# More units convolved channel-major: taps alternating on VectorE, broadcast multiplies on GpSimd

## The chip, the cores and the metric

The kernel runs on one core of one Trainium2 chip. The metric is the device time of one execution in microseconds; the executions of one kernel in the same rounds lay 0.15 to 0.65% apart, from the fastest to the slowest. Versions are compared in the same rounds on the same chip. "Step" below is one of the 768 pairs of matmul groups that make a gate and a val tile; twelve steps are a block of 512 tokens, and 48 steps, four blocks, are a unit.

## The reference

A causal depthwise convolution of seven taps, whose weights are a softmax per head, feeds a gated feed-forward block.

```python
w = exp(weight - max) ; w = w / (sum(w) + 1e-09)          # 8 heads x 7 taps
x_unf = x_pad[:, idx, :].reshape(B, S, K, H, group)       # x: 8 x 4096 x 192
out = einsum('hk,bskhg->bshg', w, x_unf)
g = out @ w_gate                                          # 192 -> 1536
silu = g * (1.0 / (1.0 + exp(-g)))
y = (silu * (out @ w_val)) @ w_out                        # 1536 -> 192
```

## The kernel before

Each step does six matmuls into a gate and a val bank (three of each), ScalarE takes the silu of gate, VectorE multiplies it by val, and TensorE multiplies the products h by w_out in groups between triples of steps ("acc").

The convolution of the next units is done beside that, in one of two ways. On TensorE, a banded matmul ("cv") is copied out as tm, written to DRAM and fetched back transposed as xc. Channel-major, a transposed load puts channels on partitions, so that a tap is a multiply by a scalar per partition. A unit takes six jobs; in the kernel before, unit 3 and every second one after it went this way:

```python
POOLED = range(3, NU, 2)
ON_DVE, ON_ACT, ON_POOL = (0, 1), (2, 3, 4), (5, 6)       # the seven taps of a job
def on_dve(k):
    nc.vector.scalar_tensor_tensor(total, shifted(k), tap[:, k:k+1],
                                   zero if k == 0 else total, op0=mult, op1=add)
def on_act(k):
    nc.scalar.activation(part, shifted(k), AF.Copy, scale=tap[:, k:k+1])
    add(part, k)                                          # GpSimd: total += part
def on_pool(k):
    nc.gpsimd.tensor_scalar(part, shifted(k), scalar1=tap[:, k:k+1], op0=mult)
    add(part, k)
# ... one ScalarE tap, and with two of three also a VectorE tap, at steps 1, 7 and 10 of a block
# ... place(): four DMA copies arrange a finished block as pxc, what the gate matmuls read
...
if n == 23:
    make_channel_taps()          # masks on VectorE, then a tap matmul on TensorE at once
```

## Time and profile before

| | before |
|---|---|
| median | 792.3 us (791.2 to 792.6) |
| TensorE / VectorE / ScalarE / GpSimd busy | 99% / 80% / 74% / 57% |
| silu starts, first of unit 0 to first of unit 1 | 60.6 us |
| a later unit, without and with convolution on TensorE | 46.9 and 48.3 us |

The lines on which the argument rests are in the prediction. What the convolution costs the helpers is in the page's costliest groups (count, busy us, mean ns of one, idle time ahead of it and what ended it):

```profile
L636 POOL TENSOR_TENSOR total<-total,part 128x512 f32<-128x512 f32 x126 | 160.1, 1270 | 225.9 <-DVE total L619 174.1
...
L649 POOL TENSOR_SCALAR piece<-x,tap_c 128x512 f32<-128x512 f16 x84 | 137.9, 1641 | 0.0
L643 ACT ACTIVATE part<-x,tap_c 128x512 f32<-128x512 f16 x126 | 89.9, 714 | 3.7 <-DMA x<-xs 3.1
...
L619 DVE SCALAR_TENSOR_TENSOR total<-x,tap_c,fill 128x512 f32<-128x512 f16 x42 | 41.1, 979 | 2.4 <-DMA x<-xs 2.4
...
L619 DVE SCALAR_TENSOR_TENSOR total<-x,tap_c,total 128x512 f32<-128x512 f16 x42 | 31.4, 748 | 3.5 <-POOL total L636 3.5
```

The two VectorE rows do the same arithmetic on the same sizes; one is 979 ns because 15 of its 42 took about 1.4 us, each of them begun inside a GpSimd add.

### The profile page before, as it was taken

Reading aid. Unit: us, or ns where it says so; the run is one execution under the profiler, and the core shown is the slowest. Engines: PE = TensorE matmul, PEld = TensorE weight load, DVE = VectorE, ACT = ScalarE, POOL = GpSimd, SP = SyncE. Lnnn points to the kernel's source line nnn. Section 1 sums busy time; section 2 is a strip of 40 time slices with the busy share of each in tenths; the row PEclk is TensorE's granted clock in tenths of the full one; section 3 lists DMA queues with packets and bytes.
Section 4 is the critical chain, followed back from the end, with each engine's and each line's share of the span. In section 5 each row is a group of like instructions: output and inputs, shape, how many; then the busy total and the mean of one; then the engine's idle time right before and its main releaser. Section 6 shows DMA issues by size and latency. Waiting matters only on the chain.

```text
span 788.7 us, 28107 instructions
## 1 busy us (share of the span) xinstructions
PE 778.3 (99%) x11563; PEld 600.3 (76%) x11563; DVE 627.3 (80%) x988; ACT 584.7 (74%) x1010; POOL 453.3 (57%) x375
## 2 busy tenths in 40 slices
PE   8898999999999999999999999999999999999998
PEld 5665678886788767887678876888678886788886
DVE  7666888688887888778897788877888788897775
ACT  6566778678777787777787687777787777786664
POOL 8204669455793658926689166873669546684000
PEclk9999999999999999999999999999999999999999
DMA  9996668653585444853557625674257652531111
GB/s 144 152 165 130 136 134 149 136 109 80 111 151 124 94 108 102 168 118 62 129 116 135 137 63 118 129 152 110 56 134 135 145 117 59 119 93 44 42 42 42
DMA packets 175970, 88.49 MB, mean 112 GB/s; under 512 B 115898, under 2 KB 175170, under 8 KB 175170
## 3 DMA queue, kind: packets, MB, share of 16 engines
q1 hardware_dynamic: 147634, 69.57, 38.3%
q0 software_dynamic: 28208, 17.13, 16.4%
q8 instruction: 90, 1.47, 0.8%
q14 instruction: 38, 0.31, 0.1%
HBM read 34.26 MB, written 39.37 MB: 93 GB/s over the span
## 4 chain that ended last, share of the span: by engine, by line
PE 96%; SPq 1%; ACT 1%; DVE 0%; DMA 0%; issue 0%; ACTq 0%
PE gate L740 51%; PE acc L766 32%; PE val L740 11%; PE cv L462 1%; SPq L498 1%; PE warm L841 1%; SPq L520 0%; PE turn L431 0%; DMA x<-xs 0%; PE cv L373 0%; ACT sig L749 0%; PE acc L787 0%; DVE h L751 0%; ACT tme L391 0%; ACT wide L331 0%
## 5 line engine op out<-in xcount | busy, mean ns | idle before, releaser
L751 DVE TENSOR_TENSOR h<-sig,val 128x512 f16<-128x512 f16 x768 | 503.5, 686 | 144.9 <-PE val L740 93.6
L749 ACT ACTIVATE sig<-gate 128x512 f16<-128x512 f32 x768 | 458.2, 597 | 176.1 <-PE val L740 104.0
L740 PEld LDWEIGHTS <-w 64*128 64x128 f16 x4608 | 321.8, 110 | 125.4 <-issue 2.9
L766 PEld LDWEIGHTS <-h 64*128 64x128 f16 x6096 | 275.8, 94 | 45.7 <-issue 4.0
L766 PE MATMUL acc<-wo,h 64*128 64x192 f16 x6096 | 306.1, 243 | 2.1 <-ACT sig L749 2.1
L740 PE MATMUL val<-xc,w 64*128 64x512 f16 x1296 | 306.9, 378 | 0.0
L740 PE MATMUL gate<-xc,w 64*128 64x512 f16 x1296 | 306.9, 378 | 0.0
L636 POOL TENSOR_TENSOR total<-total,part 128x512 f32<-128x512 f32 x126 | 160.1, 1270 | 225.9 <-DVE total L619 174.1
L740 PE MATMUL val<-pxc,w 64*128 64x512 f16 x1008 | 236.6, 376 | 0.0
L740 PE MATMUL gate<-pxc,w 64*128 64x512 f16 x1008 | 236.6, 376 | 0.0
L649 POOL TENSOR_SCALAR piece<-x,tap_c 128x512 f32<-128x512 f16 x84 | 137.9, 1641 | 0.0
L643 ACT ACTIVATE part<-x,tap_c 128x512 f32<-128x512 f16 x126 | 89.9, 714 | 3.7 <-DMA x<-xs 3.1
L636 POOL TENSOR_TENSOR total<-total,piece 128x512 f32<-128x512 f32 x42 | 54.2, 1290 | 3.5
L619 DVE SCALAR_TENSOR_TENSOR total<-x,tap_c,fill 128x512 f32<-128x512 f16 x42 | 41.1, 979 | 2.4 <-DMA x<-xs 2.4
L636 POOL TENSOR_TENSOR pxc<-total,piece 128x512 f16<-128x512 f32 x28 | 36.1, 1288 | 2.3
L825 DVE COPY o_sb<-acc 128x384 f32<-128x384 f32 x63 | 34.6, 549 | 0.0
L619 DVE SCALAR_TENSOR_TENSOR total<-x,tap_c,total 128x512 f32<-128x512 f16 x42 | 31.4, 748 | 3.5 <-POOL total L636 3.5
L824 ACT COPY o_sb<-acc 128x384 f32<-128x384 f32 x63 | 30.2, 479 | 0.1
L98 POOL DMA_DIRECT2D x<-in_x_dram x25 | 19.8, 800 | 13.3 <-ACT sig L749 13.1
L479 ACT CAST tm<-cv 128x480 f16<-128x480 f32 x32 | 16.3, 562 | 11.8 <-PE cv L462 11.8
L479 DVE CAST tm<-cv 128x480 f16<-128x480 f32 x32 | 19.6, 652 | 1.2
L490 POOL COPY tm<-tm 128x1280 f16<-128x1280 f16 x8 | 10.0, 1249 | 17.3 <-DVE tm L479 9.1
(68 smaller groups left out, 101.0 us busy)
## 6 DMA issues: line engine op xcount, KB each, us to landing
out_dram<-o_sb SPq DMA_DIRECT2D x63, 384.0 KB
scr<-tm SPq DMA_DIRECT2D x56, 130.0 KB
x<-x SPq DMA_DIRECT2D x14, 480.0 KB
xs<-in_x_dram POOLq DMA_DIRECT2D x7, 774.0 KB, 7.3
x<-in_x_dram POOLq DMA_DIRECT2D x11, 480.0 KB, 7.8
pxc<-pxc SPq DMA_DIRECT2D x56, 64.0 KB
pxc<-y SPq DMA_DIRECT2D x56, 64.0 KB
x<-in_x_dram POOLq DMA_DIRECT2D x7, 468.0 KB, 6.0
```

Of the source, the lines that this page charges most:

```text
L98: nc.gpsimd.dma_start(out=t[p0 + i0 : p0 + i1, w0 - at : w1 - at, :], in_=bass.AP(tensor=x_flat.tensor, offset=(t0 + size * w0 - pad + i0) ...
L479: eng(tm[u][:, NG * r : NG * r + NG, 2 * grp * hp : 2 * grp * hp + 2 * grp].rearrange("p g (t e) -> p g t e", t=2), banks[r][:, 0 : 2 * w] ...
L619: nc.vector.scalar_tensor_tensor(total.rearrange("p (s e) -> p s e", s=SUBS) if k == 0 else total, shifted(k).rearrange("p (s e) -> p s e" ...
L636: nc.gpsimd.tensor_tensor(dst if k == K - 1 else total, total, part, op=ALU.add)
L643: seq(nc.scalar.activation(part, shifted(k), AF.Copy, scale=tap[:, k : k + 1]))
L649: nc.gpsimd.tensor_scalar(part, shifted(k), scalar1=tap[:, k : k + 1], scalar2=None, op0=ALU.mult,)
L740: nc.tensor.matmul(o, w16[m][p0 : p0 + Q, k, e::E], xc[b][k][p0 : p0 + Q, 0:TB], start=(k == 0), stop=(k == SL - 1),)
L749: silu[n] = seq(nc.scalar.activation(sg, g, AF.Silu)).ins
L751: seq(nc.vector.tensor_tensor(hj, sg, v, op=ALU.mult))
L766: nc.tensor.matmul(acc[b][bank][:, s, :], hj[p0 : p0 + Q, ts(2 * bank + s, P)], wo16[p0 : p0 + Q, j, :], start=(not second and j == 0 and ...
L824: seq(nc.scalar.copy(o_sb[:, 0:2, :], acc[b][0]))
L825: seq(nc.vector.tensor_copy(o_sb[:, 2:4, :], acc[b][1]))
```

## The change

The intent is to take the convolution of three more units off TensorE, and to make room by giving VectorE a third tap in every second job and GpSimd a cheaper multiply. The diff, cut to its core (left out are the buffers, of x tiles 4 to 6, total 3 to 4, part 4 to 6, piece 4 to 2, pxc0 6 to 8, pxc1 and pxc2 6 to 4; the queues that now feed VectorE and ScalarE apart; and a new rule for when a block is placed):

```diff
-    POOLED = range(3, NU, 2)
+    POOLED = (3, 4, 5, 7, 8, 9, 11, 12, 13, 15)
...
-    ON_DVE, ON_ACT, ON_POOL = (0, 1), (2, 3, 4), (5, 6)
+    SHARES = (
+        ((0, 1), (2, 3, 4), (5, 6)),
+        ((0, 1, 2), (3, 4), (5, 6)),
+    )
...
-                nc.gpsimd.tensor_scalar(
-                    part, shifted(k), scalar1=tap[:, k : k + 1], scalar2=None,
-                    op0=ALU.mult,
+                    nc.gpsimd.tensor_tensor(
+                        part,
+                        shifted(k),
+                        job["tap"][:, k : k + 1].to_broadcast([P, TB]),
+                        op=ALU.mult,
...
-        plan.setdefault(s0 - 103, []).append(
-            lambda: pending.extend((v, *job) for job in jobs)
-        )
+        plan.setdefault(s0 - (86 if v == POOLED[0] else 95), []).append(lambda: queue_jobs(v))
...
-        if n == 23:
+        if n == 24:
+            make_picks()
+        if n == 33:
             make_channel_taps()
```

More of the change, by code (lines that the diff above doesn't have):

```diff
@@ L532, with make_picks @@
     taps = {}
-    def make_channel_taps():
+    pick = {}
+    def make_picks():
         for name, first, rows in (("c01", 0, P), ("c2", P, Q)):
@@ L546, in make_channel_taps @@
             seq(nc.vector.tensor_single_scalar(low, which, 0, op=ALU.is_ge))
-            pick = small(f"pick_{name}", [H, P], fp16)
+            pick[name] = small(f"pick_{name}", [H, P], fp16)
             seq(
                 nc.vector.scalar_tensor_tensor(
-                    pick, which, float(grp), low, op0=ALU.is_lt, op1=ALU.mult
+                    pick[name], which, float(grp), low, op0=ALU.is_lt, op1=ALU.mult
                 )
             )
+    def make_channel_taps():
+        for name in pick:
             bank = ppool.tile([P, TB], fp32, tag="gate", name="ctap")
@@ L556, in make_channel_taps @@
                     nc.tensor.matmul(
-                        bank[:, 0:K], pick, split[:, a, 0:K, 0],
+                        bank[:, 0:K], pick[name], split[:, a, 0:K, 0],
                         start=(a == 0), stop=(a == 1),
@@ L591, in turn_x @@
         tag = f"x{at // Q}"
-        t = cpool.tile([P, TB + XP], fp16, tag=tag, name=tag, bufs=4)
+        t = cpool.tile([P, TB + XP], fp16, tag=tag, name=tag, bufs=6)
         seq(nc.sync.dma_start_transpose(out=t, in_=rows[:, at : at + P]))
@@ L597, in join_x @@
         seq(nc.sync.dma_start(out=x12[u, i + 2][0:Q], in_=x12[u, i][Q:P]))
-    ON_DVE, ON_ACT, ON_POOL = (0, 1), (2, 3, 4), (5, 6)
-    def conv_job(u, what, i):
-        if what == "pair":
-            dst = y2[u, i] = cpool.tile([P, TB], fp16, tag="y2", name="y2", bufs=4)
-            src, tap = x12[u, i + 2], taps["c2"]
-        else:
-            t = cpool.tile([P, XW], fp16, tag="pxc0", name="pxc0", bufs=6)
-            xc[UB * u + i] = [t]
-            dst = t[:, 0:TB]
-            src, tap = x01[u, i], taps["c01"]
-        total = cpool.tile([P, TB], fp32, tag="total", name="total", bufs=3)
-        at = XP - pad
-        def shifted(k):
-            return src[:, at + k : at + k + TB]
-        def on_dve(k):
-            zero = fill.unsqueeze(1).to_broadcast([P, SUBS, P])
+    SHARES = (
+        ((0, 1), (2, 3, 4), (5, 6)),
+        ((0, 1, 2), (3, 4), (5, 6)),
+    )
@@ new lines, with conv_job, open_job, add @@
+    on_dve = []
+    on_act = []
+    finished = {}
+    started = []
+    def conv_job(n_job, u, what, i):
+        dve_taps, act_taps, pool_taps = SHARES[n_job % len(SHARES)]
+        job = {"dve": len(dve_taps), "act": len(act_taps), "parts": []}
+        at = XP - pad
+        def open_job():
+            if what == "pair":
+                y2[u, i] = cpool.tile([P, TB], fp16, tag="y2", name="y2", bufs=4)
+                job.update(dst=y2[u, i], src=x12[u, i + 2], tap=taps["c2"])
+            else:
+                t = cpool.tile([P, XW], fp16, tag="pxc0", name="pxc0", bufs=8)
+                xc[UB * u + i] = [t]
+                job.update(dst=t[:, 0:TB], src=x01[u, i], tap=taps["c01"])
+            job["total"] = cpool.tile([P, TB], fp32, tag="total", name="total", bufs=4)
+        def shifted(k):
+            return job["src"][:, at + k : at + k + TB]
+        def add(part, k):
+            total = job["total"]
+            seq(
+                nc.gpsimd.tensor_tensor(
+                    job["dst"] if k == K - 1 else total, total, part, op=ALU.add
+                )
+            )
+        def proceed():
+            if job["dve"]:
+                return
+            while job["parts"]:
+                add(*job["parts"].pop(0))
+            if job["act"]:
+                return
+            for k in pool_taps:
+                part = cpool.tile([P, TB], fp32, tag="piece", name="piece", bufs=2)
+                seq(
+                    nc.gpsimd.tensor_tensor(
+                        part,
+                        shifted(k),
+                        job["tap"][:, k : k + 1].to_broadcast([P, TB]),
+                        op=ALU.mult,
+                    )
+                )
+                add(part, k)
+            finished[u, what, i] = True
+        def dve_step(k):
+            if "total" not in job:
+                open_job()
+            total, x_k, other = job["total"], shifted(k), job["total"]
+            if k == 0:
+                total = total.rearrange("p (s e) -> p s e", s=SUBS)
+                x_k = x_k.rearrange("p (s e) -> p s e", s=SUBS)
+                other = fill.unsqueeze(1).to_broadcast([P, SUBS, P])
@@ L618, in on_dve @@
             seq(
                 nc.vector.scalar_tensor_tensor(
-                    total.rearrange("p (s e) -> p s e", s=SUBS) if k == 0 else total,
-                    shifted(k).rearrange("p (s e) -> p s e", s=SUBS)
-                    if k == 0
-                    else shifted(k),
-                    tap[:, k : k + 1],
-                    zero if k == 0 else total,
-                    op0=ALU.mult,
-                    op1=ALU.add,
-                )
-            )
-        def part_tile(name):
-            return cpool.tile([P, TB], fp32, tag=name, name=name, bufs=4)
@@ L634, in add @@
-        def add(part, k):
-            seq(
-                nc.gpsimd.tensor_tensor(
-                    dst if k == K - 1 else total, total, part, op=ALU.add
-                )
-            )
-        def on_act(k):
-            part = part_tile("part")
-            seq(nc.scalar.activation(part, shifted(k), AF.Copy, scale=tap[:, k : k + 1]))
-            add(part, k)
-        def on_pool(k):
-            part = part_tile("piece")
-            seq(
-                nc.gpsimd.tensor_scalar(
-                    part, shifted(k), scalar1=tap[:, k : k + 1], scalar2=None,
-                    op0=ALU.mult,
-                )
-            )
-            add(part, k)
@@ L656, in step, with act_step @@
-        def step(a):
-            if a < len(ON_DVE):
-                on_dve(ON_DVE[a])
-            on_act(ON_ACT[a])
-            if a == len(ON_ACT) - 1:
-                for k in ON_POOL:
-                    on_pool(k)
-        return [lambda a=a: step(a) for a in range(len(ON_ACT))]
+                    total, x_k, job["tap"][:, k : k + 1], other,
+                    op0=ALU.mult, op1=ALU.add,
+                )
+            )
+            job["dve"] -= 1
+            proceed()
+        def act_step(k):
+            if "total" not in job:
+                open_job()
+            part = cpool.tile([P, TB], fp32, tag="part", name="part", bufs=6)
+            seq(
+                nc.scalar.activation(
+                    part, shifted(k), AF.Copy, scale=job["tap"][:, k : k + 1]
+                )
+            )
+            job["act"] -= 1
+            job["parts"].append((part, k))
+            proceed()
@@ L666, in place @@
+        on_dve.extend(lambda k=k: dve_step(k) for k in dve_taps)
+        on_act.extend(lambda k=k: act_step(k) for k in act_taps)
     def place(u, i):
@@ L669, in place @@
             xc[b].append(
-                cpool.tile([P, XW], fp16, tag=f"pxc{k}", name=f"pxc{k}", bufs=6)
+                cpool.tile([P, XW], fp16, tag=f"pxc{k}", name=f"pxc{k}", bufs=4)
             )
@@ L685, with queue_jobs @@
     plan = {}
-    pending = []
-    started = []
-    finished = set()
+    jobs_made = []
     placing = []
+    def queue_jobs(u):
+        for what, i in (
+            ("block", 0), ("pair", 0), ("block", 1), ("pair", 1),
+            ("block", 2), ("block", 3),
+        ):
+            conv_job(len(jobs_made), u, what, i)
+            jobs_made.append((u, what, i))
+        placing.extend((u, i) for i in range(UB))
     def planned(v):
@@ L700, in planned @@
             plan.setdefault(s0 + off, []).append(lambda i=i: join_x(v, i))
-        jobs = [("block", 0), ("pair", 0), ("block", 1), ("pair", 1)]
-        jobs += [("block", 2), ("block", 3)]
-        plan.setdefault(s0 - 103, []).append(
-            lambda: pending.extend((v, *job) for job in jobs)
-        )
-    def pooled_work(n, room):
-        while room:
-            if not started:
-                if not pending:
-                    break
-                u, what, i = pending.pop(0)
-                started.append((u, what, i, conv_job(u, what, i)))
-            u, what, i, steps = started[0]
-            steps.pop(0)()
-            room -= 1
-            if not steps:
-                started.pop()
-                finished.add((u, what, i))
-                for q in range(UB):
-                    need = {(u, "block", q), (u, "pair", q % 2)}
-                    if need <= finished and (u, what, i) in need:
-                        placing.append((n + 14, u, q))
-        while placing and placing[0][0] <= n:
-            _, u, q = placing.pop(0)
-            place(u, q)
+        plan.setdefault(s0 - (86 if v == POOLED[0] else 95), []).append(lambda: queue_jobs(v))
+    def pooled_work(n, room):
+        if room:
+            if on_dve:
+                on_dve.pop(0)()
+            if on_act:
+                on_act.pop(0)()
+        while placing:
+            u, i = placing[0]
+            need = (u, "block", i), (u, "pair", i % 2)
+            for job in need:
+                if finished.get(job) is True:
+                    finished[job] = n
+            if not all(job in finished for job in need):
+                break
+            if n < max(max(finished[job] for job in need) + 12, ustep * u + NCH * i - 16):
+                break
+            placing.pop(0)
+            place(u, i)
     hbuf = {}
@@ L895 @@
             job()
-        pooled_work(n, 0 if work else {1: 1, 7: 1, 10: 1}.get(j, 0))
+        pooled_work(n, j in (1, 7, 10) and not work)
         if u + 1 < NU and not pooled(u + 1):
```

## The prediction

> **What bounds the kernel now.** I read the page from the top: busy times, chain, then groups. TensorE is busy 99% of the span, and the chain that ended last is TensorE for 96% of it.
>
> ```profile
> PE 778.3 (99%) x11563; PEld 600.3 (76%) x11563; DVE 627.3 (80%) x988; ACT 584.7 (74%) x1010; POOL 453.3 (57%) x375
> PE 96%; SPq 1%; ACT 1%; DVE 0%; DMA 0%; issue 0%; ACTq 0%
> ```
>
> So work taken off VectorE, ScalarE or GpSimd gains nothing by itself. Only three things shorten the run: TensorE instructions removed, TensorE waits removed, and the clock lost behind such waits. The chain in order of time gives the pace of the middle. These are equal places of successive blocks of 12 steps:
>
> ```profile
> 154.70 0.99 PE acc L766 x24
> ...
> 166.43 0.99 PE acc L766 x24
> ...
> 178.80 0.99 PE acc L766 x24
> ...
> 191.17 0.99 PE acc L766 x24
> ...
> 202.90 0.99 PE acc L766 x24
> ```
>
> A block without convolution takes 11.73 us, one that carries half a unit's convolution on TensorE takes 12.37. A unit of 48 steps that is convolved on TensorE therefore costs 2 x 0.64 = 1.28 us more than one convolved channel-major on the other engines. No channel-major unit shows an excess, so the other engines now hide all of theirs.
>
> The list of waits by engine has two real TensorE waits, and windows around them show more than the wait itself:
>
> ```profile
> PE acc L766 <- ACT sig L749: 2.1, 1, 2.1
> PE ctap L556 <- DVE pick_c L549: 1.8, 1, 1.8
> ...
> 36.00:39.00 3.00, 1.04 (x14) 0.36 (x8) 1.49 (x6) 0.67 (x2) 0.98 (x2) 1.00 0.94 94
> 39.00:43.00 4.00, 3.87 (x40) 1.89 (x48) 1.10 (x3) 1.45 (x4) 0.00 (x0) 0.57 1.60 126
> 63.00:66.00 3.00, 0.90 (x12) 0.25 (x8) 0.80 (x2) 1.28 (x3) 0.37 (x1) 1.00 0.41 90
> 66.00:70.00 4.00, 4.00 (x46) 2.85 (x48) 2.50 (x4) 1.77 (x4) 2.15 (x2) 0.58 0.66 99
> ```
>
> After the window's length the columns are busy time of PE, PEld, DVE, ACT and POOL, then the granted clock. TensorE stands still inside the first and third window, and the window after each has a clock of 0.57 and 0.58. The first stop is the tap matmul at step 23, waiting for masks that VectorE had only just made. The second is at step 43: ScalarE's first channel-major multiply waited 3.1 us for a transposed load and held up the silu behind it.
>
> [...] 3.4 us of half clock behind each of the two stops (0.57 of 4 us is 3.4 at a half and 0.6 at full).
> [...]
>
> ```profile
> L619 DVE SCALAR_TENSOR_TENSOR total<-x,tap_c,fill x42: 744/747/1409, 64.7 to 703.5; 128x512 f32<-128x512 f16 x42
> ...
> 204.16 1.40 DVE L619 SCALAR_TENSOR_TENSOR total<-x,tap_c,fill 128x512 f32<-128x512 f16 x1
> ...
> 203.75 1.27 POOL L636 TENSOR_TENSOR total<-total,piece 128x512 f32<-128x512 f32 x1
> 205.00 2.00 POOL L649 TENSOR_SCALAR piece<-x,tap_c 128x512 f32<-128x512 f16 x1
> ```
>
> The VectorE tap started inside a GpSimd add and took 1.40 instead of 0.75 us; the GpSimd multiply behind them took 2.00 instead of 1.56. But a tap that starts late in a GpSimd multiply still takes 0.75. h<-sig,val (val in PSUM) stays at 669 to 690 ns: not touched.
> [...] the one-input TENSOR_SCALAR takes 1641 ns, the two-input add 1270.
>
> **The change part by part.**
> 1. *Ten channel-major units instead of seven.* Units on TensorE after the first fall from 8 to 5. Removed: 3 x 64 matmuls with their weight loads, worth 3 x 1.28 = 3.8 us on the path. Their evictions (12 each of 0.65 us on VectorE and 0.56 on ScalarE) go too, off the path.
> 2. *Masks made at step 24, taps at step 33.* The wait of 1.8 + 0.2 us and its half clock, (1 - 0.57) x 4 = 1.7 us, go: 3.7. Against it: the taps use two of three gate banks in the middle of a triple of steps, and a bank comes free only when its silu is done, about 1.4 us after the step's start, where steps follow at 0.65. I charge 0.7 us (estimate).
> 3. *First channel-major jobs from step 58, not 41.* The transposes are issued at step 33 and will have landed. The 2.1 us wait and its half clock, (1 - 0.58) x 4 = 1.7, go: 3.8.
> 4. *VectorE.* 60 jobs x 2.5 taps = 150 scalar_tensor_tensor instead of 84. While it is behind, h instructions start 0.60 apart (three in 1.87, the last 0.67), an o_sb copy holds it 0.47 and a tap about 0.70. Twelve steps: 12 x 0.60 + 0.47 + 3 x 0.70 = 9.8 of 11.73 us. That leaves 1.9 us, or 0.65 for each tap to wait for GpSimd. An add seems to exclude a tap for some 1.07 of its 1.25 us (204.16 + 1.40 - 0.75 = 204.8, against its start at 203.75), so a tap that falls at random into back-to-back adds waits 1.07 x 1.07 / 2 / 1.25 = 0.46, and with GpSimd free part of the time 0.3. So VectorE comes to about 10.7 of 11.73: 91%, still below TensorE. One bad tap, 1.07 late, is about what three gate/val buffers absorb; I allow 0.5 us for the rare pile-up.
> 5. *GpSimd.* Two jobs now need 5 + 4 adds and 4 multiplies, 13 two-input operations at 1.27 us (I take the multiply by a broadcast tap to cost what an add costs: estimate) = 16.5 us, plus some 1.5 waiting for taps = 18. Two jobs need five slots, and three come per 12 steps: 20 steps = 19.5 us. GpSimd is 92% busy inside a group, but not on the path: counting slots in the program, a block's jobs end 29 to 71 steps before TensorE reads it.
> 6. *ScalarE.* Still one multiply per slot: 150 instead of 126, 24 x 0.71 = 17 us more, less 7 of evictions; 75%.
> 7. *Transposed loads.* Six buffers for three units in a row. In the built order one load (unit 5's last, step 155) must wait for a job whose last slot is at 154, so the queue is held some 8 steps; the next placement, step 164, is 16 before its use. Hidden.
>
> Sum: -3.8 - 3.7 + 0.7 - 3.8 + 0.5 = -10.1. Counted by silu starts, the two stops delay the steps by 8.2 rather than 7.5 us, so a little more may come: 792.3 - 10.8 = **781.5 us**, a ratio of 0.986.
>
> **The rivals.**
> - *VectorE and GpSimd lock each other out, and VectorE becomes the bound.* For it: every GpSimd operation of a job is now two-input, and there are 150 taps. If each tap waited a whole add (1.07), 12 steps would need 9.8 + 3.2 = 13.0 us: 1.3 more over some 50 blocks, +63 us. Against it: 27 of the 42 first taps take 0.75 today (their mean of 979 ns is 27 at 746 and 15 at 1400), and GpSimd is idle between some slots. An average wait of 0.7 instead of 0.3 would cost about 8 us, giving 790.
> - *GpSimd or its loads come late and TensorE waits for a placement.* For it: 92%, and the broadcast multiply was never timed here; at 1.7 us each, GpSimd would need 19.7 of 19.5. Against it: the slack of 29 steps and more. It would need a growing backlog; perhaps +5.
> - *The stops move instead of going.* With TensorE 8 us earlier, unit 2's on-chip copy (issued at 70.8 now, needed by the matmuls of step 58) may just arrive late, or the tap matmuls may still stop TensorE: 1 to 4 us given back, giving 783 to 786.
> - *Only the removed matmuls count* and both stops return: 788.5.
>
> **Range and chances.** The runs before lie within 1.4 us, so the range is about mechanism. Best case 778 (all 12 us); with a stop returned and some lock-out 788. The 2% line is 776.5: more than all I can find, so 4% for faster. Slower needs VectorE to become the bound: 4%. Within 2%: 92%.
>
> **What would show each step right or wrong.** Blocks of channel-major units stay at 11.73 (step 4 right); longer ones with VectorE never waiting for PE mean the lock-out wins. The TensorE waits on masks and on ACT sig are gone and no window before 80 us has a clock under 1.0 but the start's (2, 3). The cv matmuls fall from 512 to 320 (1). GpSimd's mean for the multiply is near 1.27, not 1.6 (5). VectorE's taps lie between 0.75 and 1.9 us with a mean near 1.05 (4). A TensorE wait on DMA pxc would prove 5 or 7 wrong. I am wrong if TensorE shows many new short waits on h or sig inside the groups.

The lost clock in steps 2 and 3 is worked out from the window clocks of 0.57 and 0.58, the hold of a tap in step 4 from the times of the tap and the add. The sum stays -10.1 us, or -10.8 counted by silu starts.

## The result, and the profile after

The changed kernel took 786.18 us (785.21 to 787.93, four runs) beside 792.46 for the kernel before: a ratio of 0.9923, 95% interval 0.9899 to 0.9947. On a second chip it was 0.9948 (0.9935 to 0.9962). Ratios here are the mean time of one kernel's runs over that of the other's of the same rounds, so not quite the ratio of the medians. It is faster by 0.5 to 0.8%, within the forecast range, but the gain is 4 to 6 us and not the 10.8 of the central figure.

The busy times, the two new forms of a VectorE tap, GpSimd's multiply and its commonest add, and TensorE's waits, from the page and the list of waits of the changed kernel:

```profile
PE 773.8 (99%) x11371; PEld 583.4 (74%) x11371; DVE 705.2 (90%) x1042; ACT 596.4 (76%) x1022; POOL 539.1 (69%) x459
...
L634 POOL TENSOR_TENSOR total<-total,part 128x512 f32<-128x512 f32 x150 | 198.4, 1323 | 106.6 <-DVE total L668 69.8
...
L649 POOL TENSOR_TENSOR piece<-x,tap_c 128x512 f32<-128x512 f16 x120 | 143.6, 1197 | 0.0
...
L668 DVE SCALAR_TENSOR_TENSOR total<-x,tap_c,total 128x512 f32<-128x512 f16 x90 | 93.5, 1038 | 0.0
...
L668 DVE SCALAR_TENSOR_TENSOR total<-x,tap_c,fill 128x512 f32<-128x512 f16 x60 | 80.1, 1334 | 0.0
...
PE cv L462 <- DMA x<-x: 1.3, 1, 1.3
...
PE acc L793 <- DVE h L778: 0.7, 1, 0.7
```

Both forms of tap have become longer: 748 to 1038 ns, 979 to 1334. With no idle time ahead of them (0.0), what grew is their own run time and not a wait for data. GpSimd's multiply fell from 1641 to 1197. The two waits of before, on masks and on the first load, are gone; a wait of the convolution for an on-chip copy is new. The windows that had a clock of 0.57 and 0.58 before are at full clock, and from 63 to 66 us TensorE is busy for all 3 us instead of 0.9 (columns as in the prediction):

```profile
39.00:43.00 4.00, 3.72 (x61) 2.61 (x48) 3.75 (x9) 2.89 (x6) 1.42 (x2) 1.00 2.04 147
63.00:66.00 3.00, 3.00 (x46) 2.37 (x44) 1.98 (x3) 1.79 (x3) 0.00 (x0) 1.00 0.45 91
66.00:70.00 4.00, 4.00 (x53) 2.94 (x51) 3.25 (x6) 3.51 (x7) 0.00 (x0) 1.00 0.61 131
```

The time can be read stage by stage from the silu starts in the timeline of ScalarE, which follow TensorE's pace (before, a unit without convolution on TensorE took 46.92 us by silu starts, four blocks of 11.73 by the chain):

| us | unit 0 | unit 1 | units 2 to 14 | mean tap, ns |
|---|---|---|---|---|
| before | 60.60 | 48.20 | 617.96 | 864 |
| changed, first chip | 54.31 | 49.84 | 617.98 | 1157 |
| changed, second chip | 53.83 | 52.62 | 617.87 | 1150 |

The start won 6.3 to 6.8 us, as forecast. Unit 1 gave back 1.6 to 4.4. The thirteen units in which three convolutions were taken off TensorE took exactly as long as before.

Their stalls are hard to see, as TensorE's ends are modelled and it looks busy (99%). The pace of the chain in order of time shows them. These are equal places of successive blocks of the changed kernel, around its worst one:

```profile
506.08 0.99 PE acc L793 x24
...
517.81 0.99 PE acc L793 x24
...
530.56 0.99 PE acc L793 x24
...
542.29 0.99 PE acc L793 x24
```

The middle block took 12.75 instead of 11.73 us with no matmul added. VectorE and GpSimd at that time, from the two timelines:

```profile
524.55 3.07 DVE L668 SCALAR_TENSOR_TENSOR total<-x,tap_c,fill 128x512 f32<-128x512 f16 x1
527.55 1.87 DVE L778 TENSOR_TENSOR h<-sig,val 128x512 f16<-128x512 f16 x3
...
524.24 0.55 POOL L583 DMA_DIRECT2D xs<-in_x_dram  x1
524.79 1.28 POOL L634 TENSOR_TENSOR total<-total,part 128x512 f32<-128x512 f32 x1
526.03 1.04 POOL L649 TENSOR_TENSOR piece<-x,tap_c 128x512 f32<-128x512 f16 x1
```

The tap starts while GpSimd issues a DMA, then stays out through a whole add and nearly all of a multiply: 3.07 us for 0.75 of work. The three h behind it are late, and TensorE waits 0.7 us for the first. This is the only one of the 150 taps that missed two turns; why it did is not shown. Elsewhere in the groups the excess is 0.1 to 0.3 us at a time, in a dozen blocks, and 0.2 to 0.3 on five of the six remaining convolution halves. Together it is 4.2 us.

Silu starts set step by step against those of a_nomult (below) show where it comes from. Of the 14 taps that were 0.8 to 1.1 us late at step 1 of a block, 13 cost TensorE 0.1 to 0.3 us each, 2.1 in all. The same delay at step 7 cost nothing in nine of twelve cases; the other three were the tap of 3.07 us (1.0) and two in blocks with convolution (0.2 each).

### The profile page after: what moved, and what is told of

The parts are those of the page before. It is cut to its first block, busy times and chain, and to the rows that moved or that the text cites. A ratio compares the mean times of both kernels' runs of the same rounds, so it can differ in the third digit from the quotient of the medians.

```text
span 783.3 us, 28008 instructions
## 1 busy us (share of the span) xinstructions
PE 773.8 (99%) x11371; PEld 583.4 (74%) x11371; DVE 705.2 (90%) x1042; ACT 596.4 (76%) x1022; POOL 539.1 (69%) x459
## 4 chain that ended last, share of the span: by engine, by line
PE 93%; SPq 3%; DMA 2%; DVE 1%; issue 1%; POOL 1%; ACT 0%; DVEq 0%; POOLq 0%
PE gate L767 35%; PE acc L793 31%; PE val L767 26%; SPq L498 1%; SPq L520 1%; DMA x<-x 1%; DMA w<-in_moe_w_val_dram 1%; DVE h L778 1%; PE cv L462 1%; SPq L598 1%; POOL w L168 0%; PE acc L814 0%; POOL xe L98 0%; PE cv L373 0%; PE turn L431 0%
## 5 line engine op out<-in xcount | busy, mean ns | idle before, releaser
L767 PE MATMUL gate<-pxc,w 64*128 64x512 f16 x1440 | 338.5, 376 | 0.0
L767 PE MATMUL val<-pxc,w 64*128 64x512 f16 x1440 | 337.0, 376 | 0.4
L634 POOL TENSOR_TENSOR total<-total,part 128x512 f32<-128x512 f32 x150 | 198.4, 1323 | 106.6 <-DVE total L668 69.8
L767 PE MATMUL gate<-xc,w 64*128 64x512 f16 x864 | 203.8, 376 | 0.5 <-ACT tap_c L567 0.5
L767 PE MATMUL val<-xc,w 64*128 64x512 f16 x864 | 203.5, 376 | 0.7 <-DMA w<-in_moe_w_val_dram 0.3
L649 POOL TENSOR_TENSOR piece<-x,tap_c 128x512 f32<-128x512 f16 x120 | 143.6, 1197 | 0.0
L668 DVE SCALAR_TENSOR_TENSOR total<-x,tap_c,total 128x512 f32<-128x512 f16 x90 | 93.5, 1038 | 0.0
L634 POOL TENSOR_TENSOR total<-total,piece 128x512 f32<-128x512 f32 x60 | 80.4, 1340 | 4.7
L668 DVE SCALAR_TENSOR_TENSOR total<-x,tap_c,fill 128x512 f32<-128x512 f16 x60 | 80.1, 1334 | 0.0
L634 POOL TENSOR_TENSOR y<-total,piece 128x512 f16<-128x512 f32 x20 | 27.4, 1372 | 1.6
```

What stands on the lines that cost most here:

```text
L634: nc.gpsimd.tensor_tensor(job["dst"] if k == K - 1 else total, total, part, op=ALU.add)
L649: nc.gpsimd.tensor_tensor(part, shifted(k), job["tap"][:, k : k + 1].to_broadcast([P, TB]), op=ALU.mult,)
L668: nc.vector.scalar_tensor_tensor(total, x_k, job["tap"][:, k : k + 1], other, op0=ALU.mult, op1=ALU.add,)
L767: nc.tensor.matmul(o, w16[m][p0 : p0 + Q, k, e::E], xc[b][k][p0 : p0 + Q, 0:TB], start=(k == 0), stop=(k == SL - 1),)
```

## The experiments

Two theories stood against each other. **A**: the whole gain lies in the first 60 steps; in the middle, the matmuls saved are paid back. **B**, the prediction's sum: the saved matmuls are worth most of 3.8 us. And for the cause of a payback: **L**, GpSimd holds VectorE's two-input taps up; **C**, VectorE simply has too many taps. All runs have five rounds.

### b_newstart: the new start in the kernel before

```diff
 (kernel before)
-        if n == 23:
+        if n == 24:
+            make_picks()
+        if n == 33:
             make_channel_taps()
-        plan.setdefault(s0 - 103, []).append(
+        plan.setdefault(s0 - (86 if v == POOLED[0] else 103), []).append(
```

> The kernel before with the new start alone (masks at step 24, tap matmuls at step 33, first channel-major jobs from step 58); still seven channel-major units and the old jobs. Theory A (the whole gain of the change lies in the first 60 steps, the three further units gave nothing net): 785 to 787 us, as fast as the changed kernel; unit 0 takes about 54.3 us of silu starts instead of 60.6, the later units alternate 46.9 and 48.3 as before. Theory B (the prediction's sum: matmuls removed are worth 3.8 us): 789 us or more, as some 4 us of the gain would be missing.

Measured: 787.8 us, ratio 0.9962 (0.9943 to 0.9982); 788 lies between the two expectations, and the time alone decides nothing. The stages do better: unit 0 took 53.84 us, so the start's gain of 6.8 is there without any other part of the change. Unit 1 gave back 2.0 (the convolution waited 1.7 us for its on-chip copy) and units 2 to 14 took 619.7, 1.8 more than before, all of it in unit 2: there a VectorE tap waited 2.7 us for GpSimd's total, h stood behind it, and acc waited 1.2 us for h. That the old job code had too little time for its first unit is the likely reason, but was not tested apart.

### a_oldstart: the changed kernel with the old start

```diff
 (changed kernel)
-        if n == 24:
-            make_picks()
-        if n == 33:
+        if n == 23:
+            make_picks()
             make_channel_taps()
-  ... s0 - (86 if v == POOLED[0] else 95)
+  ... s0 - (103 if v == POOLED[0] else 95)
```

> The changed kernel with the old start (masks and tap matmuls together at step 23, first jobs from step 41); ten units, alternating taps and broadcast multiplies kept. Theory A: 791 to 793 us, no faster than before, because small TensorE stalls inside the groups take back the 4.0 us of the removed matmuls. Theory B: 788 to 789 us. Both expect the wait for the masks (1.8 us) back and a window with a clock near 0.57.

Measured: 799.4 us, ratio 1.0101 (1.0086 to 1.0116). Both theories missed: I had not seen that the new job code needs the later start. It runs through a job's VectorE taps sooner, reaches loads that have not landed, and VectorE stands still with h behind the tap:

```profile
DVE total L668 <- DMA x<-x: 5.2, 1, 5.2
DVE total L668 <- DMA x<-xs: 3.2, 1, 3.2
```

TensorE then waited 4.9 us for h. The waits of before were back too, 1.8 us for the masks and 2.9 (2.1 before) for the silu behind ScalarE's first multiply, and TensorE ran at half clock for 6.8 us more than before. Units 0 and 1 took 61.2 and 55.4 us. The middle, 619.4, again shows no gain over 618.0 from ten units in place of seven.

### a_seven: the changed kernel with seven units

```diff
-    POOLED = (3, 4, 5, 7, 8, 9, 11, 12, 13, 15)
+    POOLED = range(3, NU, 2)
```

> The changed kernel with seven channel-major units instead of ten (every second one), all else kept. Theory A: within 1 us of the changed kernel (785 to 787): three more units on TensorE cost 4.0 us, and the stalls inside groups of three go away. Theory B (the stalls are not the groups' doing): 789 to 790 us.

Measured: 788.4 us, ratio 0.9961 (0.9946 to 0.9976), between the two again, with unit 1 at 52.75 us behind two waits for the copy (2.5 us together) and a half-clock window (mean clock of the run 0.997, of the changed kernel 0.999). Units 2 to 14 took 619.2, against 617.9 to 618.0 with ten: in this form the three further units are worth 1.2 us net, not 3.8. Against the stall-free pace of a_nomult (next), single channel-major units lose 0.26 us in each pair of units, 1.6 in all; ten units, in groups of three, lose 4.2. So the groups make it worse, but the new job code loses some time without them.

### a_nomult: GpSimd without its last two taps (wrong result)

```diff
-            for k in pool_taps:
-                ... multiply into piece, add(part, k)
+            seq(nc.gpsimd.tensor_copy(job["dst"], job["total"]))
```

> Wrong result on purpose: the changed kernel in which GpSimd leaves out the last two taps (both multiplies and their adds; one copy of total to the output in their place). VectorE and ScalarE keep all their taps. Theory L (VectorE's taps are held by GpSimd's two-input operations, and that delays h and TensorE): the taps' mean falls from 1157 ns to below 950, the stalls inside the groups all but vanish, and the time falls by 3 to 4 us to about 782.5. Theory C (VectorE simply has too many taps): stalls and time stay, 785.5 to 786.5.

Measured: 783.3 us, ratio 0.9901 (0.9887 to 0.9915); the result is wrong, as intended. Units 2 to 14 took 613.8 us: every unit 46.92 or 48.20, without one stall. VectorE still has its 150 taps, but little holds them up: 133 take 0.75 us and 17 about 1.1, behind one of the adds that GpSimd still does, and the mean is 788 ns (minimum/median/maximum in ns, from the view of the line):

```profile
L658 DVE SCALAR_TENSOR_TENSOR total<-x,tap_c,total x90: 743/745/748, 88.7 to 703.2; 128x512 f32<-128x512 f16 x90
L658 DVE SCALAR_TENSOR_TENSOR total<-x,tap_c,fill x60: 744/747/1128, 83.4 to 694.4; 128x512 f32<-128x512 f16 x60
```

Theory C falls: the number of taps is no problem. GpSimd's work on the last two taps costs 4.1 to 4.2 us (617.87 and 617.98 less 613.80), and the matmuls taken off TensorE are worth the 4.2 us (617.96 - 613.80) that were forecast as 3.8. So theory B had the worth of the matmuls right, and theory A that it is paid back. The total fell by less than that because unit 1 took 52.9 us here.

### a_firsttap: a first tap with one SBUF input

The first tap adds a tile of zeros. It can be a plain multiply:

```diff
+            if k == 0:
+                seq(nc.vector.tensor_scalar(
+                    total, x_k, scalar1=tap, scalar2=None, op0=ALU.mult))
+            else:
                 nc.vector.scalar_tensor_tensor(total, x_k, tap, total, ...)
```

> The changed kernel with the first tap of each job on VectorE as tensor_scalar (one SBUF input) instead of scalar_tensor_tensor with a zero tile. Theory L (two SBUF inputs on VectorE are what GpSimd holds up): the first tap's mean falls from 1334 ns to under 800, units 2 to 14 lose 2 to 4 us of their 618, and the time falls by as much. If the one-input form is [...]still held up: mean over 900 and no gain. Theory C (too many VectorE instructions, whichever kind): no gain.

Measured: 781.9 us, ratio 0.9879 (0.9861 to 0.9898), where the changed kernel had 0.9948 in the same rounds. It is correct and beats both kernels.

```profile
L672 DVE SCALAR_TENSOR_TENSOR total<-x,tap_c,total 128x512 f32<-128x512 f16 x90 | 94.8, 1054 | 0.0
L666 DVE TENSOR_SCALAR total<-x,tap_c 128x512 f32<-128x512 f16 x60 | 42.4, 706 | 0.0
...
L666 DVE TENSOR_SCALAR total<-x,tap_c x60: 479/644/993, 79.3 to 690.6; 128x512 f32<-128x512 f16 x60
```

The first tap falls from about 1320 to 706 ns, the other taps stay held at 1054, and units 2 to 14 take 614.1 us. Work that took 80 us of VectorE and now takes 42 gives back 3.7 of the 4.1 us. But the new form is held just like the old one, as the branch between the two theories has it (though not with its mean over 900 and no gain): 38 of the 60 took longer than the free 0.48 us, up to 0.99. If a held tap's work is taken to be as long as a free tap's, it starts 1.08 us after the start of the add that holds it, in the new form as in the old. So one SBUF input did not let a tap past GpSimd here (38 of 60 held). The gain comes from a tap of 0.48 instead of 0.75 us and from fewer and shorter holds (55 of the 60 were held in the changed kernel); the two were not separated. The rest of the gain over the changed kernel of the same rounds is unit 1 (49.6 against 52.6 us), which the edit does not touch and which differs from run to run.

### after_again and a_earlydup: the new wait in unit 1

The changed kernel was run again as the yardstick of these rounds, unaltered.

> The changed kernel unaltered, as the yardstick on this chip: ratio to before 0.991 to 0.994, units 2 to 14 adding up to about 618 us of silu starts, a wait of cv for the copy x<-x of 1 to 3 us at step 58.

Measured: 787.6 us, ratio 0.9948, just above the expected range. The wait for the copy was 2.8 us here, and a half-clock window followed, which the first run's 1.3 us had not set off (window 75 to 80 us, clock 0.66):

```profile
75.00:80.00 5.00, 3.42 (x55) 2.11 (x56) 1.22 (x2) 1.26 (x3) 1.25 (x1) 0.66 0.72 150
```

So the middle repeats within 0.1 us, and unit 1 takes 49.8 or 52.6 us. a_earlydup issues that copy earlier:

```diff
-            if ls == (37 if u == 0 else 26):
+            if ls == (32 if u == 0 else 26):
                 dup_x(u + 2)
```

> The changed kernel with unit 2's on-chip copy x<-x issued at step 32 instead of 37, ahead of three transposes. Theory (the convolution of step 58 reaches TensorE before the copy has landed, only because the start became 8 us shorter): the wait of cv for DMA x<-x goes, the second unit falls from 49.8 us or more (52.8 where the clock halves behind the wait) to about 48.2, and the time by 1.6 to 4.6 us against the changed kernel. Rival (the on-chip copy is slow because other traffic delays it, whenever it is issued): the wait stays above 1 us.

Measured: 784.1 us, ratio 0.9902 (0.9885 to 0.9919). The wait for the copy is gone, but another has come in its place, further on in the same queue:

```profile
PE gate L767 <- DMA xc<-scr: 2.0, 2, 1.8
...
113.03 0.37 PE L767 MATMUL gate<-xc,w 64*128 64x512 f16 x1 [1.75 <-DMA xc<-scr]
```

At 113 us this is step 96, the first block of unit 2. Unit 1 takes 50.6 us instead of the expected 48.2, but with no half-clock window (mean clock 0.999) the time falls by 3.5 us against the changed kernel, within the expected 1.6 to 4.6. The rival that the copy itself is slow falls.

### a_first_dup and a_best: both, and the transposes later

a_first_dup joins the two edits. a_best also issues the transposed loads of unit 3 four steps later, behind the fetch that I took for the late one:

```diff
+        late = 4 if v == POOLED[0] else 0
-            plan.setdefault(s0 + off, []).append(lambda i=i, at=at: turn_x(v, i, at))
+            plan.setdefault(s0 + off + late, []).append(lambda i=i, at=at: turn_x(v, i, at))
   (and the same for join_x)
```

> Both edits together: the first tap as tensor_scalar and the early copy. If both theories hold their gains add, 4 to 8 us under the changed kernel: 778 to 782 us, faster than both kernels.

> The changed kernel with the first tap as tensor_scalar, unit 2's copy at step 32, and unit 3's transposes and joins four steps later, so that the second block of unit 1 is fetched before them. Theory (the early copy only moved the wait to the fetch of that block, because the transposes of unit 3 stood in front of it in the one queue): neither cv on x<-x nor gate on xc<-scr waits; unit 1 takes 48.2 to 48.5 us instead of 49.6 to 52.8, and the time is 779 to 781 us. Rival (the traffic of the start, not the queue's order, is short): a wait of 1 us or more shows up in another place and the time stays at 782.

Measured: 782.1 us, ratio 0.9874 (0.9855 to 0.9893), and 782.0, ratio 0.9879 (0.9860 to 0.9898): no faster than a_firsttap alone. The gains did not add. In a_first_dup gate waits 2.3 us for fetches, in a_best 1.5, both at step 96 again:

```profile
PE gate L771 <- DMA xc<-scr: 1.5, 1, 1.5
```

The expectation for a_best failed: unit 1 took 49.9 us, not 48.5. It had put the late fetch at the second block of unit 1, step 60, where no wait stands in any of the three traces; so the edit moved transposes that had nothing to do with the wait. All three versions moved it from step 58 to 96 and left 1.5 to 2.3 us of it. Whether the queue's issue time or the traffic behind it is short in the first 100 us stays open.

### a_scalarmult: GpSimd's old multiply

```diff
-                    nc.gpsimd.tensor_tensor(part, shifted(k), tap.to_broadcast([P, TB]), op=ALU.mult)
+                    nc.gpsimd.tensor_scalar(part, shifted(k), scalar1=tap, scalar2=None, op0=ALU.mult)
```

> The changed kernel with GpSimd's multiplies as tensor_scalar with the tap as pointer scalar, as before the change. 120 multiplies take about 1.6 instead of 1.04 to 1.2 us, 50 to 60 us more of GpSimd. If the broadcast form matters, GpSimd fills the groups (over 95%), its backlog grows and taps wait longer: 788 us or more. If GpSimd has room enough, the time stays within 1 us of the changed kernel; if a one-input multiply holds VectorE's taps less, their mean falls below 1100 ns and the time by 1 to 2 us.

Measured: 790.3 us, ratio 0.9983 (0.9964 to 1.0002): the broadcast form is worth 4.3 us in units 2 to 14 (622.3 against 618.0). The taps are held less, 1063 ns in the mean, as one branch expected: 44 taps met a tensor_scalar multiply; the ten that began up to 0.23 us after its start were held, the four begun just before it and the 30 begun 0.49 us or more after it took 0.75 us. The twelve units other than unit 9 are together even 1.15 us faster than in the changed kernel. But GpSimd is now 93% busy (97 to 570 us), and its backlog outlasts the slack of the placements once, in unit 9, and a window of half clock follows (mean clock of the run 0.998); that unit takes 54.2 us instead of 48.7:

```profile
L649 POOL TENSOR_SCALAR piece<-x,tap_c 128x512 f32<-128x512 f16 x120 | 205.6, 1713 | 0.0
...
PE gate L765 <- DMA pxc<-pxc: 1.0, 1, 1.0
```

This is the prediction's second rival, and it came at the 1.7 us for which it was named.

## Why the prediction was right or wrong

The range held. The central figure was 4.7 us low (786.2 against 781.5), and two of its terms make up most of the miss. On the second chip 787.6 us lay just inside the end of the range, 788.

- **Step 1, removed matmuls, -3.8: right.** With the hold-ups away the middle fell by 4.2.
- **Steps 2 and 3, the two stops, -3.7 + 0.7 - 3.8: right.** Both waits and their half clock went; unit 0 fell by 6.3 to 6.8, and the step with the tap matmuls lost 0.8 for the 0.7 charged. The 0.7 us that the central figure adds from silu starts is a miscount: set against the same steps of b_newstart, the two stops delayed the starts by 7.6 us, not 8.2.
- **Step 4, VectorE, +0.5: the mechanism was right and the size was wrong; it measured +4.1.** The mean tap came to 1.16 us for the 1.05 expected, which is near. What failed is "one bad tap, 1.07 late, is about what three gate/val buffers absorb". That held at step 7 of a block, but not at step 1, where 13 taps that were 0.9 to 1.1 us late cost 2.1 us together; one tap that came 2.3 us late cost 1.0, and five losses in the convolution blocks another 0.9. Why steps 1 and 7 differ was not tested. The average load (96% busy in the groups, held time included) left room, but a single late tap at the wrong step still cost time. The rival was named with 8 us for an average wait of 0.7; a wait of 0.41 already cost half of that.
- **Step 5, GpSimd: the wrong size on the harmless side.** The multiply took 1.04 us at the median (1.20 in the mean, held time included), not 1.27; GpSimd was 84% busy in the groups for the 92% expected. Broadcasting was needed, though: with the old multiply the second rival happened.
- **Step 7: right**; no placement was late in the changed kernel. The third rival, "the stops move instead of going", gave the second missing term: the on-chip copy of unit 2 was late, as named, for 1.6 us in one run and 4.4 in another, where the clock halved behind it.
- A slip in the range: "best case 778 (all 12 us)" does not add up, as 792.3 - 12 is 780.3. And the sign named for being wrong, many short TensorE waits on h, did not show in the list of waits (0.7 and 0.3 us); the pace of the blocks was needed to see the loss.
- Not seen at all: the late start of the first jobs is a condition of the new job code, not just a repair. With the old start the change would have lost 8 us.

## What to carry to other kernels

Where the trace shows that one helper engine holds up another's instructions (here a VectorE tap of 0.75 us that began inside a GpSimd add took 1.40), count each of them with the wait that it can meet, and look at single late instructions against the depth of the buffers, not at the mean load. Where an operand is a constant, try the shorter form of the instruction: here adding a tile of zeros cost 3.7 us. And when a stop at the start is removed, look for the next thing in the same queue: here 1.6 to 4.4 of the 6.3 to 6.8 us were paid back there.

## What the traces show of the holds, the multiply and the clock

- A held tap. If its work is as long as a free one's (0.75 us), a held tap starts 1.08 us after the start of an add of 1.27, 0.84 after the start of a broadcast multiply of 1.04, and 0.48 after that of a TENSOR_SCALAR of 1.56 (ten taps of a_scalarmult): before the other instruction ends. These starts are estimates from the measured ends. Taps that began later in a TENSOR_SCALAR were not held: 13 taps of the kernel before, begun 1.10 to 1.19 us after its start, took 0.75. One tap in 150 of the changed kernel waited through an add and a multiply in a row (3.07 us).
- GpSimd's multiply. TENSOR_SCALAR with a scalar per partition (f16 in, f32 out, 128x512) took 1564 ns at the median in the kernel before, and TENSOR_TENSOR with the same scalar as a broadcast operand 1042 in the changed kernel.
- The half clock. In the kernel before, the granted clock fell to 0.5 at 39.37 and at 66.67 us, each time for 3.41 us. The falls lie 27.31 us apart, eight times 3.41, and the first is ten times 3.41 after the first recorded rise, at 5.23 us. Counted in stretches of that length from this rise, TensorE stood idle for 2.09 and 2.10 us in the two just before the falls, and for 1.09 or less in every other up to 780 us. In the changed kernel, counted likewise from 3.78 us, it was 1.34 or less, and the clock fell only at the end of the run, at 782.0. The length of a single stop does not sort them: those of 1.85 and 2.1 us (kernel before) and 2.8 (after_again) had half clock behind them, one of 1.9 (a_first_dup, mean clock 0.999) had not. What sets it off was not shown.
